# Seven groups per step, and narrow products of two units that alternate head by head

## The chip, the core and the metric

The kernel runs on one core of one Trainium2 chip. The metric is the device time of one execution in microseconds (us); less is better. Three runs of the kernel before gave a median of 929.04 us (928.44 to 930.88).

## What is computed

Inputs are q, k, v of shape (4, 8, 768, 48) (batch, heads, sequence, head dimension), beta of shape (4, 8, 768), and two weight matrices in double precision. The reference first runs the delta rule over the sequence, then a feed-forward over 3072 tokens of 384 features:

```python
k_n = k / (np.linalg.norm(k, axis=-1, keepdims=True) + 1e-06)
for t in range(S):
    y[:, :, t] = np.einsum('bhd,bhde->bhe', q[:, :, t], state)
    v_old = np.einsum('bhde,bhd->bhe', state, kt)
    state = state + bt[:, :, :, None] * np.einsum('bhd,bhe->bhde', kt, vt - v_old)
...
h = x @ w_in                              # 384 -> 2048
g = h * (1.0 / (1.0 + np.exp(-1.702 * h)))
out = (g @ w_out)                         # 2048 -> 384
```

## The kernel before

**Units and slots.** The sequence is cut into 6 chunks of 128 tokens. A *unit* is one chunk of one batch with all 8 heads; there are 24, in the order of chunks and, within a chunk, of the 4 batches. The main loop has 25 *slots*, and `slot(n, 20.8)` puts these works side by side: the second part of the step of unit n-1 (call it A) and the first part of the step of unit n (B), both from the generator `advance`; `prepare` for unit n+4; in pairs of slots one `invert` for two later units; in slots 0 to 3 the conversion of weights from double precision (`weights`); and some pieces of the feed-forward of finished units, 20.8 units of cost at 1.3 apiece, so 16 pieces. A pair of units makes 32 pieces, two slots' worth.

**A step.** A chunk is solved in 4 blocks of 32 rows. In `psR` stands what is to be taken from the values: for all rows the keys' products with the state `S_bd` (L421, four products of 128 x 96), and for block 1, 2 and 3 the products of the rows above, head by head (L430, 8 products of 32, 64 or 96 rows x 32 columns x 48). DVE subtracts the block of psR from the values `V` (L436). Then the 8 heads' block is multiplied with the inverse `XB` of the triangular system into `psU` (L438, 8 products of 32 x 32 x 48), and ACT copies it to `U` (L442). These L430 and L438 products are called narrow here, and eight of them in a row a burst. After block 3 come the new state's products (`psS`, L447), the queries' products with the old state and with U (`psY`, L456 and L462), ACT's copy to `x`, the state's update on DVE (L475), and the transposes of x into `psXT` (L481) and `xT` (L482).

**Around it.** `prepare` transposes k and q (`psT`, L285), forms the Gram matrices (`psG`, L299; rows 0 to 47 hold one head and 64 to 111 the next, and the two are multiplied in turn) and sends blocks of them through DRAM to `invert`, which inverts the triangular systems of two units on DVE (L339 to L397: a product, 15 rounds of a product and a sum, and 8 pairs of larger ones). `feed_forward` works pieces of three `ph` products (L495) for the first matrix and of two `po` products (L505) for the second. float32 products are two passes each on TensorE.

**What sets the order.** `merge` gives every work its number of items and a stretch of the slot, and takes the items in the order of their middles, one `yield` at a time. The framework then schedules each engine's instructions from that order and its own estimates; within one engine they run in the order that results. Buffers: `ps_seq` has four PSUM banks for psR, psU, psS, psY and psXT, so a fifth tile waits until one of the four has been read. While there is no feed-forward yet (slots 0 to 2), products on a constant keep TensorE busy (`warm`, L135; `warmth`: 8 times 4 per slot).

Of the kernel before, what the change touches and what calls it, by code (L numbers as in the profile page):

```python
# [8 lines left out]
F32 = mybir.dt.float32  # L9
# [3 lines left out]
ALU = mybir.AluOpType  # L13
ACT = mybir.ActivationFunctionType
# [4 lines left out]
def kernel(  # L19
# [31 lines left out]
    NB = C // BS  # L51
    HB = 2
# [76 lines left out]
    def warm(n, after=None):  # L129

        ps = ps_moe.tile([128, 256], F32, tag="moe", name="ps_warm")
        if after is not None:
            after(ps[:, 0:1], 0.0)
        for _ in range(n):
            nc.tensor.matmul(ps, lhsT=ones[:, 0:128], rhs=ones, start=True, stop=True)  # L135
# [272 lines left out]
        yield 0.0  # L408


    def advance(n, xT):
        c, b = units[n]
        kn, kqT, G = ready.pop(n)
        V = loaded.pop(n)
        XB = inverse.pop(n)
        psR = ps_seq.tile([128, H, D], F32, tag="seq", name="psR")
        psU = ps_seq.tile([128, H, D], F32, tag="seq", name="psU")
        U = wk.tile([128, H, D], F32, tag="U", name="U")
        if c > 0:
            for j in range(NP):  # L420
                nc.tensor.matmul(  # L421
                    psR[:, 2 * j : 2 * j + 2, :], lhsT=kqT[:, j, 0, :], rhs=S_bd[:, b, j],
                    start=(j == 0), stop=True, skip_group_check=True,
                )
            yield 1.0
        for blk in range(NB):
            r, above = slice(blk * BS, (blk + 1) * BS), slice(0, blk * BS)
            if blk > 0:
                for h in range(H):
                    nc.tensor.matmul(  # L430
                        psR[r, h, :], lhsT=G[above, h, 0, r], rhs=U[above, h, :],
                        start=(c == 0 and h == 0), stop=True, skip_group_check=True,
                    )
                yield 0.7
            if c > 0 or blk > 0:
                nc.vector.tensor_tensor(V[r], V[r], psR[r], op=ALU.subtract)  # L436
            for h in range(H):
                nc.tensor.matmul(  # L438
                    psU[r, h, :], lhsT=XB[r, h, :], rhs=V[r, h, :], start=True, stop=True
                )  # L440
            yield 0.7
            nc.scalar.copy(U[r], psU[r])  # L442

        if c < NC - 1:
            psS = ps_seq.tile([128, NP, 2, D], F32, tag="seq", name="psS")
            for j in range(NP):
                nc.tensor.matmul(  # L447
                    psS[:, j], lhsT=kn[:, 2 * j : 2 * j + 2, :].rearrange("p a d -> p (a d)"),
                    rhs=U[:, 2 * j : 2 * j + 2, :], start=True, stop=True,
                )  # L450

            yield 0.9
        psY = ps_seq.tile([128, H, D], F32, tag="seq", name="psY")
        if c > 0:
            for j in range(NP):
                nc.tensor.matmul(  # L456
                    psY[:, 2 * j : 2 * j + 2, :], lhsT=kqT[:, j, 1, :], rhs=S_bd[:, b, j],
                    start=(j == 0), stop=True, skip_group_check=True,
                )
            yield 0.9  # L460
        for h in range(H):
            nc.tensor.matmul(  # L462
                psY[:, h, :], lhsT=G[:, h, 1, :], rhs=U[:, h, :],
                start=(c == 0 and h == 0), stop=True, skip_group_check=True,
            )
            if h == 3:
                yield 0.9
        yield 0.9
        x = wk.tile([128, DM], F32, tag="o", name="x")
        nc.scalar.activation(x, psY.rearrange("p h d -> p (h d)"), ACT.Copy)  # L470

        if c < NC - 1:
            for hh in range(2):
                pr = slice(hh * 64, hh * 64 + 64)
                nc.vector.tensor_tensor(  # L475
                    S_bd[pr, b, :, hh, :], psS[pr, :, hh, :], S_bd[pr, b, :, hh, :], op=ALU.add
                )

        psX = ps_seq.tile([128, KC, 128], F32, tag="seq", name="psXT2")
        for j in range(KC):  # L480
            nc.tensor.transpose(psX[:, j, :], x[:, j * 128 : (j + 1) * 128], ident)  # L481
        nc.vector.tensor_copy(xT[:, :, b % HB * C : (b % HB + 1) * C], psX)  # L482
        yield 0.5


    def feed_forward(c, b0, xT):
# [47 lines left out]
    def warmth(n, k):  # L534
        for _ in range(n):
            warm(k)
            yield 0.0
# [11 lines left out]
    def merge(*works):  # L549

        order = sorted(
            (lo + (hi - lo) * (i + 0.5) / n, w)
            for w, (_, n, lo, hi) in enumerate(works) for i in range(n)
        )
        for _, w in order:
            next(works[w][0], None)
        for work, *_ in works:
            run(work)

    def run(work):  # L560
        for _ in work:
            pass

    def part(work, n):
        for _ in range(n):
            yield next(work, None)

    steps, xTs, inverting = {}, {}, {}

    def slot(n, share):  # L570

        c, b = units[n] if n < len(units) else (NC, 0)
        works = []
        if n > 0:
            works.append((steps.pop(n - 1), 8 if n > B else 7, 0.0, 1.0))
        if n < len(units):
            h = n // HB
            if b % HB == 0:
                xTs[h] = wk.tile([128, KC, NTH], F32, tag="xT", name="xT", bufs=3)
            steps[n] = advance(n, xTs[h])  # L580
            first = 5 if c > 0 else 3
            works.append((part(steps[n], first), first, 0.0, 1.0))
        if n + B < len(units):
            works.append((prepare(n + B), 4, 0.0, 1.0))
        m = n - HB
        if m >= 0 and m + B < len(units):
            if m % HB == 0:
                c1, b1 = units[m + B]
                inverting[0] = invert(c1, b1, HB)
                works.append((part(inverting[0], 13), 13, 0.3, 1.0))  # L590
            else:
                works.append((inverting[0], 13, 0.0, 0.65))
        if n < len(WB):
            works.append((weights(WB[n]), WB[n], 0.0, 1.0))
        if queue:
            works.append((take(share), max(1, round(share / 1.3)), 0.0, 1.0))
        elif n <= HB:
            works.append((warmth(8, NB0), 8, 0.0, 1.0))
        merge(*works)
        if n == len(WB) - 1:  # L600
            run(weights(n_parts))
        if n > 0:
            if n - 1 + B < len(units):
                load_values(n - 1 + B)
            m = n - 1 + len(KN)
            if m < len(units):
                load(m, ((KN, k), (QP, q)), sync if c == 0 else nc.sync.dma_start)
# [66 lines left out]
```

## Time and profile before

| | before |
|---|---|
| median of 3 runs | 929.04 us |
| the profiled execution | 928.69 us |
| its span on the core | 927.0 us |
| TensorE (PE): busy, passes | 877.7 us, 6356 |
| VectorE (DVE) busy | 495.4 us |
| ScalarE (ACT) busy | 195.4 us |
| GpSimd (POOL) busy | 100.8 us |
| mean granted TensorE clock | 0.965 |

The span is what the core's instructions cover; 1.7 us of the execution lie around it. PE counts passes of products, PEld the loads of their weights. A group's row names line, engine, operation, output and inputs, shape and count, then busy time and mean length of one in ns, then the idle time of the engine ahead of them and what ended it. Passes overlap, so the mean length of one is more than its distance from the next.

### The profile page before, as it was taken

To read this page: it belongs to the slowest core of one execution; us is meant where nothing else is said; L and a number is where in the kernel's file an instruction comes from. 1 tells how busy PE (TensorE), PEld (TensorE's weight loads), DVE (VectorE), ACT (ScalarE), POOL (GpSimd) and SP (SyncE) were. 2 spreads that over 40 slices of the span, in tenths; PEclk is the share of its full clock that TensorE was granted. 3 is DMA by queue.
4 is the path that set the end of the run, shared out by engine and by line. 5 is a ranking of instruction groups with operands and counts; after the bars stand their busy time and mean duration, and the time that the engine had idled before them with its cause. 6 is when DMAs were issued, how large, how long until landed. Compare 5 with 4: busy or idle time off the path is not lost.

```text
span 927.0 us, 14851 instructions
## 1 busy us (share of the span) xinstructions
PE 877.7 (95%) x6356; PEld 666.5 (72%) x6356; DVE 495.4 (53%) x1022; ACT 195.4 (21%) x354; POOL 100.8 (11%) x92
## 2 busy tenths in 40 slices
PE   8119999999999999999999999999999999999998
PEld 7107778678768778768768768768768768778684
DVE  7898787987591482482383383384293283110000
ACT  4103423222112212212212212212212102112020
POOL 2111030111011021011021011011000000000000
PEclk9657969999999999999999999999999999999999
DMA  9844562422212212213113113113112101000000
GB/s 232 221 53 113 151 164 51 111 64 50 58 43 50 49 48 54 46 44 60 41 46 64 37 49 63 32 37 74 29 39 48 29 23 27 5 13 1 10 9 18
DMA packets 159299, 54.55 MB, mean 59 GB/s; under 512 B 127232, under 2 KB 154880, under 8 KB 159232
## 3 DMA queue, kind: packets, MB, share of 16 engines
q1 hardware_dynamic: 153104, 52.38, 24.4%
q10 hardware_dynamic: 6128, 1.21, 0.9%
q8 instruction: 50, 0.82, 0.4%
q14 instruction: 17, 0.14, 0.1%
HBM read 33.13 MB, written 20.45 MB: 58 GB/s over the span
## 4 chain that ended last, share of the span: by engine, by line
PE 87%; DVE 10%; POOL 1%; issue 1%; ACT 0%; DVEq 0%; POOLq 0%
PE ph L495 29%; PE po L505 24%; PE psU L438 7%; PE psR L430 6%; PE psG L299 5%; PE psY L462 4%; PE ps_warm L135 3%; PE psT L285 3%; DVE P L346 2%; PE psS L447 2%; PE psY L456 2%; PE psR L421 2%; DVE A L347 1%; DVE P L101 1%; POOL rn L242 1%; DVE YB L101 1%
## 5 line engine op out<-in xcount | busy, mean ns | idle before, releaser
L495 PE MATMUL ph<-xT,w_in 128*128 128x256 f32 x1152 | 282.1, 389 | 1.6 <-DVE xT L482 1.6
L505 PE MATMUL po<-w_out,gT 128*128 128x384 f32 x768 | 279.4, 497 | 0.0
L495 PEld LDWEIGHTS ph<-xT,w_in 128*128 128x128 f32 x1152 | 210.0, 191 | 34.8 <-ACT gT L500 3.0
L505 PEld LDWEIGHTS po<-w_out,gT 128*128 128x128 f32 x768 | 135.5, 190 | 71.2 <-issue 2.3
L436 DVE TENSOR_TENSOR V<-V,psR 32x384 f32<-32x384 f32 x92 | 50.6, 550 | 182.2 <-PE psR L430 128.2
L500 ACT ACTIVATE gT<-ph 128x512 f32<-128x512 f32 x96 | 57.3, 597 | 221.4 <-PE ph L495 221.4
L442 ACT COPY U<-psU 32x384 f32<-32x384 f32 x96 | 45.1, 470 | 195.3 <-PE psU L438 194.6
L438 PEld LDWEIGHTS psU<-V,XB 32*32 32x32 f32 x1536 | 67.5, 106 | 24.7 <-issue 12.1
L438 PE MATMUL psU<-V,XB 32*32 32x48 f32 x1536 | 77.7, 205 | 0.0
L135 PE MATMUL ps_warm<-ident 128*128 128x256 bf16 x236 | 35.9, 310 | 42.3 <-DVE ps_warm L101 39.2
L430 PEld LDWEIGHTS psR<-U,G 64*32 64x32 f32 (+2 forms) x1152 | 53.5, 108 | 28.5 <-issue 19.4
L307 DVE COPY G<-psG 128x512 f32<-128x512 f32 x44 | 30.4, 690 | 70.0 <-PE psG L299 69.3
L430 PE MATMUL psR<-U,G 64*32 64x48 f32 (+2 forms) x1152 | 63.3, 206 | 0.6 <-ACT U L442 0.6
L323 POOL TENSOR_SCALAR_AFFINE_SELECT G<-G 128x1024 f32<-128x1024 f32 x24 | 33.8, 1410 | 251.5 <-DVE G L307 101.5
L135 PEld LDWEIGHTS <-ident 128*128 128x128 bf16 x236 | 25.1, 111 | 49.5 <-DVE ps_warm L101 40.2
L299 PE MATMUL psG<-kqT 48*128 48x256 f32 x384 | 59.4, 403 | 0.3
L462 PEld LDWEIGHTS psY<-U,G 128*128 128x128 f32 x384 | 51.2, 196 | 6.8
L363 DVE TENSOR_TENSOR P<-NT,YB 64x2 f32<-64x2 f32 (+4 forms) x150 | 51.0, 340 | 4.6
L299 PEld LDWEIGHTS psG<-kqT 48*128 48x128 f32 x384 | 36.6, 186 | 20.6 <-issue 15.7
L238 POOL TENSOR_TENSOR ksq<-KN 128x384 f32<-128x384 f32 x18 | 16.8, 932 | 312.3 <-DMA KN<-in_k_dram 312.3
L367 DVE TENSOR_REDUCE YB<-P 64x2 f32<-64x2 f32 (+4 forms) x150 | 48.0, 320 | 4.4
L462 PE MATMUL psY<-U,G 128*128 128x48 f32 x384 | 48.9, 272 | 0.0
(78 smaller groups left out, 687.6 us busy)
## 6 DMA issues: line engine op xcount, KB each, us to landing
Nd<-G SPq DMA_DIRECT2D x24, 512.0 KB, 3.2
w_out<-in_moe_w_in_dram SPq DMA_DIRECT2D x12, 512.0 KB, 5.1
w_out<-in_moe_w_out_dram SPq DMA_DIRECT2D x14, 384.0 KB, 3.6
KN<-in_k_dram SPq DMA_DIRECT2D x24, 192.0 KB, 2.8
V<-in_v_dram SPq DMA_DIRECT2D x24, 192.0 KB, 3.0
out_dram<-o SPq DMA_DIRECT2D x24, 192.0 KB, 1.9
QP<-in_q_dram SPq DMA_DIRECT2D x21, 192.0 KB, 3.0
NT<-Nd SPq DMA_DIRECT2D x24, 128.0 KB, 2.5
```

The costliest lines, as they stand in the source:

```text
L135: nc.tensor.matmul(ps, lhsT=ones[:, 0:128], rhs=ones, start=True, stop=True)
L299: nc.tensor.matmul(ps[hh][:, i], lhsT=kqT[pr, g + i, 0, :], rhs=kqT[pr, g + i, :, :], start=True, stop=True,)
L363: tt(P, diag(Nf, i * BS, [[0, i], [1, i]]), diag(Yf, 0, [[BS, i], [1, i]]), op=ALU.mult,)
L367: red(diag(Yf, i, [[BS, i]]), P, axis=AX.X, op=ALU.add, negate=True)
L430: nc.tensor.matmul(psR[r, h, :], lhsT=G[above, h, 0, r], rhs=U[above, h, :], start=(c == 0 and h == 0), stop=True, skip_group_check=True,)
L436: nc.vector.tensor_tensor(V[r], V[r], psR[r], op=ALU.subtract)
L438: nc.tensor.matmul(psU[r, h, :], lhsT=XB[r, h, :], rhs=V[r, h, :], start=True, stop=True)
L442: nc.scalar.copy(U[r], psU[r])
L462: nc.tensor.matmul(psY[:, h, :], lhsT=G[:, h, 1, :], rhs=U[:, h, :], start=(c == 0 and h == 0), stop=True, skip_group_check=True,)
L495: nc.tensor.matmul(ph[:, u], lhsT=w_in[:, j, f * 128 : (f + 1) * 128], rhs=xT[:, j, :], start=(j == 0), stop=(j == KC - 1),)
L500: nc.scalar.activation(gT[-1][:, f0 % FQ : f0 % FQ + 2], ph, ACT.Gelu_apprx_sigmoid)
L505: nc.tensor.matmul(po, lhsT=gT[f // FQ][:, f % FQ, i * C : (i + 1) * C], rhs=w_out[:, f, :], start=(f == 0), stop=(f == FC - 1),)
```

## The change

`advance` becomes a class `Step` with a method for each group of products, and `slot` writes out seven groups by hand, with the rest of the slot's work dealt out behind each: two items of the inversion, a seventh of what is left of the weights, and feed-forward pieces until a seventh of what is left of the 20.8 is used up (3, 3 and then 2 each) or, while there is none, 6 warm products (NB0; 4 before, and 8 times).

```diff
-    NW, NA0, NY, NB0 = 80, 3, 48, 4
+    NW, NA0, NY, NB0 = 80, 3, 48, 6
...
+        def solve(self, blk, h):
+            r = slice(blk * BS, (blk + 1) * BS)
+            nc.tensor.matmul(
+                self.psU[r, h, :], lhsT=self.XB[r, h, :], rhs=self.V[r, h, :],
+                start=True, stop=True,
+            )
...
-        works = []
-        if n > 0:
-            works.append((steps.pop(n - 1), 8 if n > B else 7, 0.0, 1.0))
...
-        merge(*works)
+        for group in range(7):
+            if group == 0:
+                if A:
+                    for h in range(H):
+                        A.above(2, h)
+                    A.rest(2)
+                if B_:
+                    B_.keys()
+                    B_.rest(0)
+                next(P, None)
+            elif group == 1:
+                for h in range(H):
+                    if A:
+                        A.solve(2, h)
+                    if B_:
+                        B_.solve(0, h)
+                if A:
+                    A.solved(2)
+                if B_:
+                    B_.solved(0)
+                next(P, None)
+            elif group == 2:
+                if A:
+                    for h in range(H):
+                        A.above(3, h)
+                    A.rest(3)
+                    A.queries()
+            elif group == 3:
+                for h in range(H):
+                    if A:
+                        A.solve(3, h)
+                    if B_:
+                        B_.above(1, h)
+                if A:
+                    A.solved(3)
+                if B_:
+                    B_.rest(1)
+                next(P, None)
+            elif group == 4:
+                if B_:
+                    for h in range(H):
+                        B_.solve(1, h)
+                    B_.solved(1)
+                if A:
+                    A.state()
+                next(P, None)
+                run(P)
+            elif group == 5:
+                if A:
+                    A.outputs()
+            elif A:
+                A.transposed()
+            ahead_of(inverting, 2)
...
+            if queue:
+                for cost in take(todo / (7 - group)):
+                    todo -= cost
+            elif n <= HB:
+                warm(NB0)
```

`above` is the product with the rows above (L430 before, L438 after), `rest` DVE's subtraction (L436, now L446), `solve` the product with the inverse (L438, now L450), `solved` ACT's copy, `keys` and `queries` the products with the state (both L427 now), `state` the new state with its update, now in one place, `outputs` psY's products with U, `transposed` the transposes. `queries` comes right behind `rest(3)`; before, it came behind the new state's products. Block 2's product with the rows above moves from unit n's first part, at a slot's end, to the next slot's first group.

PE's order in the middle of the program, before: part of a slot with psR and psU bursts, each with feed-forward products (ph) around it. A row's x is the number of equal products that follow each other, and the psU row of 16 is eight of one unit and then eight of the other.

```order
L430 MATMUL psR<-U,G 32x48 x8
L495 MATMUL ph<-xT,w_in 128x256 x6
L438 MATMUL psU<-V,XB 32x48 x16
L495 MATMUL ph<-xT,w_in 128x256 x3
L285 MATMUL psT<-ident,QP_83 128x128 x4
L495 MATMUL ph<-xT,w_in 128x256 x3
L447 MATMUL psS<-U,KN_75 128x96 x4
L495 MATMUL ph<-xT,w_in 128x256 x3
L430 MATMUL psR<-U,G 32x48 x8
L495 MATMUL ph<-xT,w_in 128x256 x3
L456 MATMUL psY<-S_bd,kqT 128x96 x4
```

Now, from the end of the second group into the fourth of a slot in the middle, with the numbers of the buffers (psU_3258 and psR_3257 are unit A's, psU_3513 and psR_3512 unit B's):

```order
L450 MATMUL psU_3258<-V_2763,XB_2993 32x48
L450 MATMUL psU_3513<-V_3017,XB_3470 32x48
L285 MATMUL psT_3566<-ident_106,QP1_83 128x128 x4
L515 MATMUL po_3541<-w_out_202,gT_3336 128x384 x2
L515 MATMUL po_3541<-w_out_202,gT_3406 128x384 x4
L438 MATMUL psR_3257<-U_3259,G_2428 32x48 x8
L515 MATMUL po_3541<-w_out_202,gT_3477 128x384 x2
L427 MATMUL psY_3593<-S_bd_117,kqT_2312 128x96 x4
L515 MATMUL po_3541<-w_out_202,gT_3477 128x384 x2
L450 MATMUL psU_3258<-V_2763,XB_2993 32x48
L438 MATMUL psR_3512<-U_3514,G_2667 32x48
```

The bursts' heads alternate between two units, the feed-forward stands in fewer and longer pieces, and psY with the state has moved ahead of psS, two po products behind the psR burst of block 3.

DVE's order around the subtractions of a slot with an inversion, before (the rounds of the inversion are L363 and L367, the larger products L346, `o` is the feed-forward's output):

```order
L363 TENSOR_TENSOR P<-NT,YB 64x338
L512 COPY o<-po 128x384
L436 TENSOR_TENSOR V<-V,psR 32x384
L367 TENSOR_REDUCE YB<-P 64x2x13
L363 TENSOR_TENSOR P<-NT,YB 64x392
L475 TENSOR_TENSOR S_bd<-psS,S_bd 64x4x48 x2
```

Now:

```order
L367 TENSOR_REDUCE YB<-P 64x2x14
L446 TENSOR_TENSOR V<-V,psR 32x384
L363 TENSOR_TENSOR P<-NT,YB 64x450
L367 TENSOR_REDUCE YB<-P 64x2x15
L346 TENSOR_TENSOR P<-NT,YB 64x1024
L346 TENSOR_TENSOR P<-NT,YB 64x768
L522 COPY o<-po 128x384
L446 TENSOR_TENSOR V<-V,psR 32x384
```

Block 3's subtraction stands behind 14 rounds of the inversion, all of them since block 0's, and block 1's behind the last round, two larger products and the copy of `o`.

More of the change, by code (lines that the diff above doesn't have):

```diff
@@ L420, in advance @@
             for j in range(NP):
                 nc.tensor.matmul(
-                    psR[:, 2 * j : 2 * j + 2, :], lhsT=kqT[:, j, 0, :], rhs=S_bd[:, b, j],
-                    start=(j == 0), stop=True, skip_group_check=True,
-                )
[L425 to L436, printed above, removed]
+                    ps[:, 2 * j : 2 * j + 2, :], lhsT=self.kqT[:, j, i, :],
@@ new lines, in queries, with state @@
+        def queries(self):
+            self.psY = self.bank("psY")
+            if self.c > 0:
+                self.with_state(self.psY, 1)
+        def state(self):
+            if self.c == NC - 1:
+                return
+            psS = self.bank("psS", (128, NP, 2, D))
+            for j in range(NP):
+                nc.tensor.matmul(
+                    psS[:, j],
+                    lhsT=self.kn[:, 2 * j : 2 * j + 2, :].rearrange("p a d -> p (a d)"),
+                    rhs=self.U[:, 2 * j : 2 * j + 2, :], start=True, stop=True,
+                )
+            for hh in range(2):
+                pr = slice(hh * 64, hh * 64 + 64)
+                St = S_bd[pr, self.b, :, hh, :]
+                nc.vector.tensor_tensor(St, psS[pr, :, hh, :], St, op=ALU.add)
@@ L437, in advance, with outputs @@
+        def outputs(self):
             for h in range(H):
                 nc.tensor.matmul(
-                    psU[r, h, :], lhsT=XB[r, h, :], rhs=V[r, h, :], start=True, stop=True
-                )
[L441 to L481, printed above, removed]
@@ L576, in slot @@
         if n < len(units):
             h = n // HB
-            if b % HB == 0:
+            if n % HB == 0:
                 xTs[h] = wk.tile([128, KC, NTH], F32, tag="xT", name="xT", bufs=3)
[L580 to L584, printed above, removed]
-        m = n - HB
[L586 to L598, printed above, removed]
-        merge(*works)
+            B_ = steps[n] = Step(n, xTs[h])
+        P = prepare(n + B) if n + B < len(units) else iter(())
+        m = n - HB
+        if m >= 0 and m % HB == 0 and m + B < len(units):
+            inverting = invert(*units[m + B], HB)
@@ new lines, in slot @@
+        left = WB[n] if n < len(WB) else 0
+        todo = share
+        for group in range(7):
[51 more added lines that the diff above has]
+            ahead_of(inverting, 2)
+            more = left // (7 - group)
+            run(weights(more))
+            left -= more
+            if queue:
[3 more added lines that the diff above has]
+                warm(NB0)
```

76 lines of the change are left out of this document (47 added, 29 removed).

## The prediction, made before the changed kernel ran

> **What bounds the kernel now.** I read the page first: busy time, then the slices.
>
> ```profile
> PE 877.7 (95%) x6356; PEld 666.5 (72%) x6356; DVE 495.4 (53%) x1022; ACT 195.4 (21%) x354; POOL 100.8 (11%) x92
> PE   8119999999999999999999999999999999999998
> DVE  7898787987591482482383383384293283110000
> PEclk9657969999999999999999999999999999999999
> ```
>
> PE is full from the fourth slice on, at the full clock from the seventh; DVE is half free behind it. The busy times by window, for one stretch of the start and one two-slot stretch of the middle (length, then busy time and count per engine, then clock, DMA share, GB/s):
>
> ```profile
> core 0: us, PE busy (x) PEld busy (x) DVE busy (x) ACT busy (x) POOL busy (x), PEclk, DMA share, GB/s
> 106.00:132.00 26.00, 24.16 (x229) 19.26 (x226) 21.64 (x55) 9.51 (x18) 5.31 (x5) 0.77 0.60 144
> 415.00:485.00 70.00, 70.00 (x518) 53.04 (x517) 36.69 (x74) 14.61 (x27) 9.34 (x8) 1.00 0.21 46
> ```
>
> In the middle PE has work in all 70.00 us. What is gained there must come out of PE's own instructions. A busy PE can still be draining or waiting for weights, so I next looked at PE's timeline around some short products ("busy" runs from the first start to the last end; the next row starts before that end):
>
> ```profile
> 494.06 1.40 PE L438 MATMUL psU<-V,XB 32*32 32x48 f32 x32
> ...
> 496.79 0.60 PE L285 MATMUL psT<-ident,QP 128*128 128x128 f32 x4
> 497.23 1.46 PE L495 MATMUL ph<-xT,w_in 128*128 128x256 f32 x6
> ...
> 499.39 1.49 PE L495 MATMUL ph<-xT,w_in 128*128 128x256 f32 x6
> 500.80 0.86 PE L430 MATMUL psR<-U,G 32*32 32x48 f32 x16
> 501.60 1.56 PE L495 MATMUL ph<-xT,w_in 128*128 128x256 f32 x6
> 503.00 1.03 PE L456 MATMUL psY<-S_bd,kqT 128*128 128x96 f32 x8
> 503.86 1.27 PE L495 MATMUL ph<-xT,w_in 128*128 128x256 f32 x5
> ```
>
> Every float32 product is two passes (x16 is 8 heads); a transpose is one. The pace of a feed-forward pass, and of two slots, comes from the chain of waits (start, length, work):
>
> ```profile
> 170.62 4.52 PE po L505 x14
> ...
> 205.14 6.48 PE ph L495 x30
> 211.62 1.33 PE psU L438 x32
> ...
> 282.37 1.33 PE psU L438 x32
> ```
>
> A ph pass takes 6.48 / 30 = 0.216 us, a po pass 4.52 / 14 = 0.323; the same burst comes back after two slots, 70.8 us. From 499.39 to 503.00 there are 3.61 us, of which twelve such passes are 2.59; so **a burst of 8 narrow products costs 1.02 us** with its way in and out. Its own passes: (0.86 - 0.20) / 15 = 0.044 us apart, taking 0.20 us for the last pass from the groups below, so some 0.70 us is passing and 0.32 us is the way in and out. A burst of 16 products, A's eight and then B's eight, is busy 1.40 instead of 0.86: 0.54 us more, hence **1.56 us**. That is less than sixteen more passes at 0.044 (0.70): where the second unit's products, in other rows and columns of the array, follow the first's, some passes ran beside each other.
>
> ```profile
> L438 PE MATMUL psU<-V,XB 32*32 32x48 f32 x1536 | 77.7, 205 | 0.0
> L430 PE MATMUL psR<-U,G 64*32 64x48 f32 (+2 forms) x1152 | 63.3, 206 | 0.6 <-ACT U L442 0.6
> ```
>
> The narrow products hold PE for 141 us of 927, and more with the switching.
>
> **Does taking turns work?** The change has the heads of two units alternate over the whole burst. The nearest thing in the trace is psG, whose heads alternate between rows 0 to 47 and 64 to 111 of the array already:
>
> ```profile
> 505.28 1.13 PE L299 MATMUL psG<-kqT 48*128 48x256 f32 x8
> L299 PE MATMUL psG<-kqT 48*128 48x256 f32 x384 | 59.4, 403 | 0.3
> ```
>
> Eight passes of 256 columns, the size of a ph pass, start within 1.13 - 0.40 = 0.73 us, 0.10 apart on average, where ph's are 0.216 apart. Two groups of rows each run at the full pace when their products alternate in fours of load and pass. I carry that over to the narrow bursts: 16 alternating products last as long as 8, plus one small offset: **1.03 us**, an estimate from the 1.02 row. Its passes are five times shorter than psG's, and that is what the first rival is about.
>
> **The burst term.** Counted over PE's whole order, before: 122 bursts of 8, 23 of 16. After: 90 of 8 and 39 alternating ones (21 of two units' block solves, 18 of a solve with the other unit's block product; in the first slots the scheduler has pulled some pairs apart). Before 122 x 1.02 + 23 x 1.56 = 160.3; after 90 x 1.02 + 39 x 1.03 = 132.0. **-28.3 us**, nearly all of it on the path, since PE sets the end.
>
> **Small wide groups** (psR, psY and psS of four products, the transposes). They lie less often behind feed-forward passes, and more often behind a burst or each other. A burst's way out is already in the 1.02. What is left is that their first weights aren't loaded under a long pass. The psY group above, behind a ph pass, takes 0.86 us (503.00 to 503.86), 0.108 a pass. I put a quarter of a pass, 0.03 us, on two groups in each of 20 slots: **+1.2**, an estimate, bounds 0 and 3.
>
> **Warm-up products.** Slots 0 to 2 get 7 x 6 instead of 8 x 4, 30 more.
>
> ```profile
> L135 PE MATMUL ps_warm<-ident 128*128 128x256 bf16 x236 | 35.9, 310 | 42.3 <-DVE ps_warm L101 39.2
> ```
>
> 35.9 / 236 = 0.152 each, 4.6 us if all stand on the path, 0 if all fall into waits of the first steps; I take **+2.3**.
>
> **The wait for xT.**
>
> ```profile
> L495 PEld LDWEIGHTS ph<-xT,w_in 128*128 128x128 f32 x1152 | 210.0, 191 | 34.8 <-ACT gT L500 3.0 <-DVE xT L482 2.6 <-DVE P L363 0.7
> ```
>
> Where a new pair of units enters the feed-forward, ph waits 2.6 us in all for the copy of xT. After, the transposes are the seventh group, and behind them come four po products, block 2's burst, the state product and the transposes of the next step (8 x 0.323 + 1.02 + 0.86 + 0.44 = 4.9 us) before the first ph. **-2.6**, bounds -2.6 and 0.
>
> **The wait that is added.** psY's products with the state now stand two ph (or po) products behind block 3's burst, and take a fifth bank of a pool of four, the one that psR has until DVE's subtraction has read it. All of PE queues behind that psY. The pace without DVE being late, from the timeline of DVE behind the 500.80 burst:
>
> ```profile
> 501.70 0.55 DVE L436 TENSOR_TENSOR V<-V,psR 32x384 f32<-32x384 f32 x1 [9.77 <-PE psR L430]
> ```
>
> It ended at 502.25, 0.65 after the next ph's start at 501.60. Two ph products are four passes, 0.86 us; two po products 1.29. So 0 us, with 0.2 us to spare behind ph and 0.6 behind po. If DVE comes late that cover is gone; the case is below. The other hand-overs to DVE and ACT have two or three pieces behind them, 2.6 us and more. That XB is ready: as before, DVE's order has a pair's whole inversion done a slot ahead of its use; the loads moved past on SP stay as many as they were and cost nothing.
>
> **The start.** Slots 0 to 3 hang on the steps' own hand-overs, on weight conversion in DVE (21.64 of 26.00 us above) and on a clock of 0.77. Seven strict groups may go better or worse there: 26 x 0.23 = 6 us is what a full clock would give; I take 0, bounds -6 and +6.
>
> **Sum.** -28.3 + 1.2 + 2.3 - 2.6 = -27.4. The profiled execution took 928.7 (span 927.0 and 1.7 around it): 901.3. The median of the runs is 0.35 above it: **901.6 us**. With all bounds at their good ends -36.9, 892; at their bad ends -14.7, 914.
>
> **Rivals.** *Passes come too slowly to fill two row groups.* The fastest sequence of narrow passes that the trace holds is the second half of the x32 burst, 0.54 / 16 = 0.034 us on average. If that were the least spacing, an alternating burst would be busy 0.20 + 31 x 0.034 = 1.25 us instead of 0.87: 39 x 0.38 = 14.8 more, 916. For it: nothing here shows 32 narrow passes at 0.022. Against it: psG's heads come in the same turns, loads and passes of one before those of the other, and still run level. 0.14.
> The Trainium skill has a rule of this kind (TensorE: Matmul & The Clock Gate, "Wait — 56ns, not 53.3ns?"): starts never come closer than some 25 ns however short the product; an estimate by it is 39 x 32 x 3 ns = 4 us more, 905. The x32 row neither bears it out nor excludes it.
>
> *Alternating gains no more than standing side by side.* Then the 39 cost 1.56: 39 x 0.53 = 20.7 more, 922. Against it psG. 0.06.
>
> *DVE becomes the bound in every second slot, and the time is longer.* One pair's inversion is worked in one slot:
>
> ```profile
> L363 DVE TENSOR_TENSOR P<-NT,YB 64x2 f32<-64x2 f32 (+4 forms) x150 | 51.0, 340 | 4.6
> L367 DVE TENSOR_REDUCE YB<-P 64x2 f32<-64x2 f32 (+4 forms) x150 | 48.0, 320 | 4.4
> L346 DVE TENSOR_TENSOR P<-A,NT 64x256 f32<-64x256 f32 (+3 forms) x40 | 33.6, 861 | 1.2
> L346 DVE TENSOR_TENSOR P<-NT,YB 64x1024 f32<-64x1024 f32 (+3 forms) x40 | 33.4, 858 | 0.3
> L347 DVE TENSOR_REDUCE YB<-P 64x64 f32<-64x256 f32 (+3 forms) x40 | 31.6, 810 | 0.4
> L347 DVE TENSOR_REDUCE A<-P 64x64 f32<-64x1024 f32 (+3 forms) x40 | 31.5, 810 | 0.4
> L397 DVE TENSOR_TENSOR YS<-YB,bI 64x1024 f32<-64x1024 f32 (+1 forms) x11 | 13.4, 1216 | 0.2
> L339 DVE TENSOR_TENSOR NT<-NT,bI 64x1024 f32<-64x1024 f32 x10 | 12.2, 1219 | 0.3
> ```
>
> 229.1 / 10 + 1.2 + 1.2 = 25.3 us of the 36.7 in two slots; with half of the rest, 31.0 us in a slot that shall shrink from 35.4 to about 33.9. There are ten such slots, all with po pieces. The decisive place is block 3's subtraction, ahead of psY. From block 0's subtraction on DVE has 14 rounds, at most 14 x 0.66 = 9.2 us; PE has 24 po passes (7.8), two groups of transposes (0.9) and two bursts (2.05), 10.7, less some 0.8 until block 0's subtraction is done: 9.9. Only 0.7 to spare, and the 0.6 behind po. If DVE came 2.7 us later than that cover allows in each of the ten slots, the 27.4 would be gone; from there on it is slower than before, 932 with 3 us. For it: the small margins and an in-order queue. Against it: 31.0 is under 33.9, and before, with as much to do in 35.4, V mostly found DVE waiting:
>
> ```profile
> L436 DVE TENSOR_TENSOR V<-V,psR 32x384 f32<-32x384 f32 x92 | 50.6, 550 | 182.2 <-PE psR L430 128.2
> ```
>
> 0.07.
>
> *The time does not move, or the groups don't come as written* (the scheduler undoes them, or the start loses what the middle gains): the order shows the turns in 39 bursts, so 0.03.
>
> **Numbers.** The forecast as worked out has 0.70. The range goes from 890, a little below the good ends, to 917, which takes in the 914 and the slow feed's 916; outside lie the side-by-side case, the two last and a remnant, some 0.17. A measurement of this kernel tells about 0.3% (2.8 us) from no change. Faster by more: 0.70 + 0.14 + 0.06, less a little for a start gone badly, 0.88; within it 0.03; slower 0.09.
>
> **What would show it.** Right: in the timeline after, psU bursts of x32 busy about 0.9 us instead of 1.40; two slots in about 67.7 us where they took 70.8; the narrow groups' busy time near 112 us (90 x 0.86 + 39 x 0.87) where it was 141; no waits of psY on V. Slow feed: x32 bursts of 1.0 to 1.25. DVE bound: idle time of PE's psY or psU put down to V in every second slot, and DVE without idle time ahead of V there. Wrong altogether: two slots of 70 us or more with x32 bursts at 1.4.

## The result, and the profile after

| | before | after |
|---|---|---|
| median | 928.74 us (4 runs, 925.15 to 930.88) | 891.23 us (4 runs, 887.91 to 894.75) |
| profiled execution, its span | 928.69, 927.0 us | 889.75, 888.0 us |
| mean granted clock | 0.965 | 0.974 |

The ratio is 0.960 (95% interval 0.955 to 0.965): 37.5 us less by the medians, 39.0 by the two spans. The forecast was 901.6, range 890 to 917.

From the page of the changed kernel, busy times and then the slices of DVE and of the clock:

```profile
PE 841.3 (95%) x6386; PEld 638.2 (72%) x6386; DVE 491.2 (55%) x1022; ACT 194.8 (22%) x354; POOL 99.8 (11%) x92
DVE  7889689978781771671681681681681570110000
PEclk9659999999999999999999999999999999999999
```

PE still sets the end. Two things differ: its clock is at 90% or more (a 9) in every slice from the fourth on, where before it was so from the seventh, and DVE's full and empty slots alternate more sharply in the middle (6 to 8 and 1, before 8 and 2 to 4).

The stretches of the start and of the middle that were shown of before, and then two stretches of a slot's length, the first with most of an inversion:

```profile
core 0: us, PE busy (x) PEld busy (x) DVE busy (x) ACT busy (x) POOL busy (x), PEclk, DMA share, GB/s
106.00:132.00 26.00, 26.00 (x280) 21.58 (x280) 21.14 (x61) 12.23 (x21) 7.23 (x6) 1.00 0.69 182
415.00:485.00 70.00, 70.00 (x552) 53.29 (x550) 38.02 (x76) 15.79 (x29) 9.39 (x8) 1.00 0.22 50
424.00:458.00 34.00, 34.00 (x252) 23.81 (x251) 26.32 (x57) 6.49 (x12) 4.89 (x4) 1.00 0.17 41
458.00:491.60 33.60, 33.60 (x271) 27.54 (x270) 10.99 (x18) 8.23 (x15) 5.00 (x5) 1.00 0.30 63
```

In the same 70 us PE starts 552 passes where it started 518, and DVE has 26.32 us of work in the stretch with most of the inversion, 10.99 in the other. The chain of waits gives the period of two slots:

```profile
363.45 3.87 PE po L515 x12
...
430.54 3.87 PE po L515 x12
```

The same po pieces come back after 67.09 us (70.8 before). Why is seen in PE's timeline, through the second, third and the beginning of the fourth group of one slot:

```profile
501.44 0.87 PE L450 MATMUL psU<-V,XB 32*32 32x48 f32 x32
...
506.69 0.87 PE L438 MATMUL psR<-U,G 96*32 96x48 f32 x16
507.49 1.56 PE L515 MATMUL po<-w_out,gT 128*128 128x384 f32 x4
508.89 1.03 PE L427 MATMUL psY<-S_bd,kqT 128*128 128x96 f32 x8
...
511.61 0.20 PE L450 MATMUL psU<-V,XB 32*32 32x48 f32 x1
511.62 0.20 PE L438 MATMUL psR<-U,G 32*32 32x48 f32 x1
511.65 0.20 PE L450 MATMUL psU<-V,XB 32*32 32x48 f32 x1
511.66 0.20 PE L438 MATMUL psR<-U,G 32*32 32x48 f32 x1
```

The psU burst of 32 passes at 501.44 is busy 0.87 us where it was 1.40; sixteen passes of one unit alone (506.69) take the same 0.87. The last four rows are the inside of an alternating burst: a pass of unit A and a pass of unit B start 0.01 us apart, and the next two 0.04 later, so each unit goes at its own 0.04 and they go side by side.

Where the 39 us went is read from the first and last start of the feed-forward passes. The rows of ph and po seen by tile (count, least, median and longest ns, first and last start in us), first of before:

```profile
L495 PE MATMUL ph<-xT,w_in x1152: 379/379/793, 132.1 to 902.7; 128*128 128x256 f32 x192
L505 PE MATMUL po<-w_out,gT x768: 486/486/590, 166.4 to 923.2; 128*128 128x384 f32 x192
```

and of after:

```profile
L505 PE MATMUL ph<-xT,w_in x1152: 378/379/484, 123.1 to 863.7; 128*128 128x256 f32 x192
L515 PE MATMUL po<-w_out,gT x768: 485/486/591, 156.6 to 884.2; 128*128 128x384 f32 x192
```

From the first ph to the last po it is 791.1 us before and 761.1 after: **-30.0**. The first ph comes 9.0 us earlier: **-9.0**. From the last po to the span's end it is 3.8 in both.

### The profile page after: what moved, and what is told of

Read it like the earlier page. It is cut to its first block, busy times and chain, and to the rows that moved or that the text cites. A ratio compares the mean times of both kernels' runs of the same rounds, so it can differ in the third digit from the quotient of the medians.

```text
span 888.0 us, 14915 instructions
## 1 busy us (share of the span) xinstructions
PE 841.3 (95%) x6386; PEld 638.2 (72%) x6386; DVE 491.2 (55%) x1022; ACT 194.8 (22%) x354; POOL 99.8 (11%) x92
## 4 chain that ended last, share of the span: by engine, by line
PE 93%; DVE 5%; DMA 1%; issue 0%; POOL 0%; ACT 0%; SPq 0%; DVEq 0%
PE ph L505 29%; PE po L515 29%; PE psU L450 7%; PE psG L299 6%; PE psR L438 5%; PE psY L481 5%; PE ps_warm L135 3%; PE psT L285 3%; PE psS L469 2%; PE psR L427 2%; PE psY L427 2%; DVE P L101 1%; PE psXT L491 1%; DVE YB L101 1%; DVE z L101 1%; DVE tmp L101 1%
## 5 line engine op out<-in xcount | busy, mean ns | idle before, releaser
L505 PE MATMUL ph<-xT,w_in 128*128 128x256 f32 x1152 | 268.2, 383 | 0.0
L515 PE MATMUL po<-w_out,gT 128*128 128x384 f32 x768 | 268.0, 493 | 0.0
L446 DVE TENSOR_TENSOR V<-V,psR 32x384 f32<-32x384 f32 x92 | 50.7, 551 | 167.3 <-PE psR L438 160.1
L450 PEld LDWEIGHTS psU<-V,XB 32*32 32x32 f32 x1536 | 54.7, 105 | 30.6 <-issue 19.0
L438 PEld LDWEIGHTS psR<-U,G 64*32 64x32 f32 (+2 forms) x1152 | 52.6, 107 | 21.3 <-issue 20.0
L323 POOL TENSOR_SCALAR_AFFINE_SELECT G<-G 128x1024 f32<-128x1024 f32 x24 | 29.0, 1210 | 338.5 <-DVE G L307 180.0
L450 PE MATMUL psU<-V,XB 32*32 32x48 f32 x1536 | 64.9, 203 | 0.0
L438 PE MATMUL psR<-U,G 64*32 64x48 f32 (+2 forms) x1152 | 62.3, 205 | 0.0
L363 DVE TENSOR_TENSOR P<-NT,YB 64x2 f32<-64x2 f32 (+4 forms) x150 | 48.7, 325 | 4.8 <-DVE YB L367 0.3
L367 DVE TENSOR_REDUCE YB<-P 64x2 f32<-64x2 f32 (+4 forms) x150 | 48.0, 320 | 4.7
L481 PEld LDWEIGHTS psY<-U,G 128*128 128x128 f32 x384 | 46.9, 193 | 3.6
L493 DVE COPY xT<-psXT 128x384 f32<-128x384 f32 x24 | 13.2, 552 | 64.1 <-PE psXT L491 64.0
L286 ACT ACTIVATE kqT<-psT 128x512 f32<-128x512 f32 x48 | 27.9, 593 | 85.5 <-PE psT L285 85.4
L481 PE MATMUL psY<-U,G 128*128 128x48 f32 x384 | 45.5, 272 | 0.0
L522 DVE COPY o<-po 128x384 f32<-128x384 f32 x24 | 13.3, 555 | 53.8 <-PE po L515 53.4
```

The costliest lines, as they stand in the source:

```text
L363: tt(P, diag(Nf, i * BS, [[0, i], [1, i]]), diag(Yf, 0, [[BS, i], [1, i]]), op=ALU.mult,)
L367: red(diag(Yf, i, [[BS, i]]), P, axis=AX.X, op=ALU.add, negate=True)
L438: nc.tensor.matmul(self.psR[r, h, :], lhsT=self.G[a, h, 0, r], rhs=self.U[a, h, :], start=(self.c == 0 and h == 0), stop=True, skip_group_ ...
L446: nc.vector.tensor_tensor(self.V[r], self.V[r], self.psR[r], op=ALU.subtract)
L450: nc.tensor.matmul(self.psU[r, h, :], lhsT=self.XB[r, h, :], rhs=self.V[r, h, :], start=True, stop=True,)
L481: nc.tensor.matmul(self.psY[:, h, :], lhsT=self.G[:, h, 1, :], rhs=self.U[:, h, :], start=(self.c == 0 and h == 0), stop=True, skip_group_ ...
```

## The experiments

All kernels do the whole computation. Except for e4 and e9, which change the kernel before, each changes the changed kernel. "First to last" is from the first ph to the last po of the profiled execution. The half clock is worked out from the windows, twice (1 - PEclk) times 20 us, over 75 to 135 us.

| | median us (runs) | first ph | last po | first to last | half clock |
|---|---|---|---|---|---|
| before | 928.74 (4) | 132.1 | 923.2 | 791.1 | 22.0 |
| after | 891.23 (4) | 123.1 | 884.2 | 761.1 | 3.6 |
| e1_side | 913.41 (4) | 126.4 | 907.7 | 781.3 | 10.4 |
| e2_cool | 905.27 (4) | 139.2 | 899.9 | 760.7 | 38.8 |
| e3_side_cool | see there | 139.0 | 926.4 | 787.4 | |
| e4_warm_before | 928.34 (10) | 130.5 | 923.0 | 792.5 | 10.4 |
| e5_by2 | 894.69 (2) | 123.1 | 885.0 | 761.9 | 3.6 |
| e6_by4 | 899.40 (2) | 123.1 | 893.8 | 770.7 | 3.6 |
| e7_split | 898.67 (2) | 121.4 | 890.9 | 769.6 | 0 |
| e8_swap | 887.32 (6) | 122.8 | 882.1 | 759.3 | 3.6 |
| e9_before40 | 932.02 (10) | 133.2 | 925.9 | 792.7 | 16.4 |
| e10_swap_warm8 | 891.10 (4) | 126.8 | 884.9 | 758.1 | 0 |

The first theory: the 30 us of the middle are the forecast's terms, the turns above all. Its rival: the turns are worth little, and the regrouping or something else gives the gain. For the 9 us of the start the question was whether the clock gives them, and what gives the clock.

**e1: the seven groups stay, the turns go.** In the second and fourth group, A's eight products and then B's eight:

```diff
-                for h in range(H):
+                for h0 in range(0, H, 8):
                     if A:
-                        A.solve(2, h)
+                        for h in range(h0, h0 + 8):
+                            A.solve(2, h)
                     if B_:
-                        B_.solve(0, h)
+                        for h in range(h0, h0 + 8):
+                            B_.solve(0, h)
...
```

> The changed kernel with the turns undone: in the second and fourth group unit A's eight products come first and then unit B's eight; all else as changed. Theory 1 (the turns bring the gain): each of the 39 bursts costs 1.56 us again instead of about 1.03, so 20.7 us more than 891.2, about 912. Rival (the seven groups with longer feed-forward stretches bring it, the turns little): not over 896.

Measured 913.41 us (910.20 to 915.82), 0.982 of before (0.978 to 0.986). The rows of ph and po by tile:

```profile
L505 PE MATMUL ph<-xT,w_in x1152: 378/379/484, 126.4 to 887.2; 128*128 128x256 f32 x192
L515 PE MATMUL po<-w_out,gT x768: 485/486/591, 160.4 to 907.7; 128*128 128x384 f32 x192
```

Its timeline in the middle:

```profile
514.28 1.40 PE L450 MATMUL psU<-V,XB 32*32 32x48 f32 x32
```

The burst is back at 1.40, and first to last is 781.3, **20.2 us** more than after (the forecast: 20.7; by the medians it is 22.2, since the first ph comes 3.3 us later too, with 10.4 us of half clock in place of 3.6). So the turns are worth 20.2 of the 30.0 us in the middle, and the rest of the change, with 16 bursts fewer (145 to 129) and no wait for xT, 791.1 - 781.3 = **9.8** (the forecast: 28.3 - 20.7 - 1.2 + 2.6 = 9.0). The first theory holds.

**e2: fewer warm products, about as many as before.**

```diff
-                warm(NB0)
+                warm(4 + group % 2)
```

> The changed kernel with 4 or 5 warm products behind a group, 31 in a slot as against 42 (32 before the change). Theory 2 (more warm products keep the TensorE clock up in the first slots, and that gave what the forecast had at 0): the trace shows half clock for 10 to 20 us again between 85 and 137 us, and the time rises by 5 to 10 us, to 896 to 901. Rival (the seven groups hand over faster whatever the clock): within 3 us of 891.

Measured 905.27 (904.62 to 909.23), ratio 0.974 (0.971 to 0.978): 14.0 over after, more than was expected. First to last is after's, 760.7; all of it lies in the start, whose windows show the granted clock in the third column behind the length:

```profile
core 0: us, PE busy (x), PEclk, DMA share, GB/s
95.00:115.00 20.00, 20.00 (x141) 0.53 0.43 114
115.00:135.00 20.00, 20.00 (x127) 0.50 0.26 58
```

PE is as busy as ever, at half the clock. The seven groups with 31 warm products per slot do worse in the start than the order of before with 32; with 42 they do far better. The extra warm products, forecast as a cost of 2.3, are a gain of 14 in this order, by the medians.

**e3: e1 and e2 together,** to see whether the two gains add up.

```diff
-                for h in range(H):
+                for h0 in range(0, H, 8):
...
-                warm(NB0)
+                warm(4 + group % 2)
```

> Both undone: no turns, and 31 warm products in a slot. If the two parts add, 20.7 + 5 to 10 above 891.2: 917 to 922, and what is left to the 928.7 of before is the regrouping alone, 7 to 12 us. Rival (they don't add, since without turns PE is busier and stays warm): about 912, as with the turns alone undone.

The four runs, 910.4, 925.7, 931.5 and 932.0 us, had mean clocks of 0.973, 0.956, 0.949 and 0.949, so that their median (928.59) isn't used. The one at 0.973 took about as long as e1 (913.41, its four at 0.970 to 0.976): in that run, which has no trace, 31 warm products did not cost e2's 14 us. So their number doesn't settle by itself whether the clock drops. In the profiled run, the one of 932.0 us, a second stretch at half clock, about 208 to 222 us, lengthens first to last to 787.4. Counting feed-forward passes in the trace, from the 271st to the last one it is 667.9 us, as in e1 (before 678.8, after 649.2). So behind the start the two changes don't touch each other; for the whole time e3 is inconclusive.

**e4 and e9: the kernel before, with more warm products.** If their number alone sets the clock, the order of before should win those 9 us too.

```diff
-    NW, NA0, NY, NB0 = 80, 3, 48, 4
+    NW, NA0, NY, NB0 = 80, 3, 48, 6
```

> The kernel before with 6 instead of 4 products at each of the 8 warm places, 48 in a slot. Theory 2 (the clock): full clock from about 100 us on, and 5 to 10 us less than 928.7: 919 to 924. Rival (the groups, not the clock, made the start shorter): the same time or up to 4 us more for 48 more products.

e9 has 5 in place of 6, so 40 per slot, near after's 42.

```diff
-    NW, NA0, NY, NB0 = 80, 3, 48, 4
+    NW, NA0, NY, NB0 = 80, 3, 48, 5
```

> The kernel before with 5 instead of 4 products at each of its 8 warm places, 40 in a slot against 42 in the changed kernel. Theory (the number of warm products alone sets the clock and with it the first feed-forward pass): half clock under 10 us in all between 75 and 140 us, the first feed-forward pass at 123 to 126 us, 6 to 9 us less than 928.7. Rival (it takes the seven groups as well, since with 48 the order of before still came to its first pass only at 130.5): first pass at 129 to 132, the time within 3 us of before.

e4 measured 928.34 (ratio 0.998, 0.996 to 1.001), e9 932.02 (1.004, 1.001 to 1.006). No gain in either. The window from 115 to 135 us, of before:

```profile
115.00:135.00 20.00, 18.16 (x118) 0.62 0.58 135
```

of e4:

```profile
115.00:135.00 20.00, 19.37 (x140) 0.74 0.47 107
```

of e9:

```profile
115.00:135.00 20.00, 19.01 (x132) 0.59 0.39 94
```

and of after:

```profile
115.00:135.00 20.00, 20.00 (x182) 1.00 0.71 188
```

The number alone falls as a theory. In the timeline the last warm products and the first ph stand like this in e9:

```profile
115.17 0.72 PE L135 MATMUL ps_warm<-ident 128*128 128x256 bf16 x5
...
133.17 1.22 PE L495 MATMUL ph<-xT,w_in 128*128 128x256 f32 x2
```

and in after:

```profile
121.11 0.82 PE L135 MATMUL ps_warm<-ident 128*128 128x256 bf16 x6
...
123.14 4.05 PE L505 MATMUL ph<-xT,w_in 128*128 128x256 f32 x18
```

In e9 (and before) 17 us of short products and small waits follow the last warm product, and the clock is down in them; the new code deals six out behind every group, to 1.2 us before the first ph. Some of e4's come as late as 125.8, and it still has 0.74, so "late enough" isn't the whole condition either.

**e5 and e6: turns of two and of four heads.** If PE only has to see both units' products somewhere ahead, all are equal; if only a few passes can wait while the other unit's go on, by fours loses most.

```diff
-                for h in range(H):
+                for h0 in range(0, H, 2):
                     if A:
-                        A.solve(2, h)
+                        for h in range(h0, h0 + 2):
+                            A.solve(2, h)
...
```

This is e5, in both groups as in e1; e6 has 4 in place of 2.

> The changed kernel with turns of two heads instead of one (A's two, B's two, and so on), all else the same. Theory (PE lets some passes of the one unit wait in their rows while it passes on those of the other; before, B's first pass ran beside the last three of A): four passes in a turn fit nearly, so the alternating psU burst takes 0.80 to 0.87 us to the next group, and from the first feed-forward pass to the end at most 2 us more than after. Rival (products run side by side however far apart they stand): exactly as after. Rival (only strict turns of one head work): 8 us and more.

> Turns of four heads. Theory of few waiting passes: eight passes in a turn no longer fit, so a part of each turn runs alone; the alternating psU burst takes 1.0 to 1.1 us, and from the first feed-forward pass to the end it is 8 to 11 us more than after. Rival (any distance): as after. Rival (only one head): as with A's eight and B's eight, 20 us more.

e5 measured 890.52 and 898.85, e6 899.32 and 899.47 (ratios 0.962, 0.955 to 0.969, and 0.967, 0.961 to 0.973). Two runs each decide little; the traces do. One burst in the timeline of e5:

```profile
501.77 0.89 PE L450 MATMUL psU<-V,XB 32*32 32x48 f32 x32
```

and one in that of e6:

```profile
505.98 1.12 PE L450 MATMUL psU<-V,XB 32*32 32x48 f32 x32
```

All 39 alternating bursts of a trace last the same, in both 0.02 us over the upper end of what was expected. First to last grows by 0.8 us for twos and 9.6 for fours, where 39 bursts of 0.25 us more make 9.8. With all 32 passes one behind the other a burst would take 0.87 + 16 x 0.042 = 1.54 us, an estimate from the row of 16 passes (506.69, after) and from what its second eight add to e7's row of eight below, (0.87 - 0.53) / 8. With one change of unit it is 1.40, with three 1.12: each change lets 0.14 us pass side by side, some three passes. The fourth group of a slot of e6 shows them, A's psU and B's psR; the program has eight passes of A first, then eight of B:

```profile
515.96 0.40 PE L450 MATMUL psU<-V,XB 32*32 32x48 f32 x5
516.15 0.23 PE L438 MATMUL psR<-U,G 32*32 32x48 f32 x1
516.19 0.20 PE L450 MATMUL psU<-V,XB 32*32 32x48 f32 x1
...
516.28 0.20 PE L450 MATMUL psU<-V,XB 32*32 32x48 f32 x1
```

B's first pass starts behind five of A's, and A's last three (516.19, 516.24, 516.28) start after it. The theory of few waiting passes holds. By it the estimate is 0.56 for seven changes, below the 0.87 that one unit needs by itself, which is why twos (0.89) are nearly as good as ones (0.87).

**e7: one burst cut in two,** block 3's product with the rows above, with a feed-forward piece between the halves. It measures what a way into and out of a burst costs.

```diff
                     for h in range(H):
+                        if h == H // 2 and queue:
+                            todo -= next(queue[0], 0) or 0
                         A.above(3, h)
```

> The changed kernel with block 3's burst cut in two halves of four heads with one feed-forward piece between them. Theory of the forecast's sum (a burst's way in and out costs 0.32 us): in about 20 slots one more way in and out, so 6 to 8 us more from the first feed-forward pass to the end. Rival (the way in and out is hidden, only passes count): 0.

Measured 896.44 and 900.90. In the timeline the cut burst stands as

```profile
509.30 0.53 PE L438 MATMUL psR<-U,G 96*32 96x48 f32 x8
509.76 1.56 PE L515 MATMUL po<-w_out,gT 128*128 128x384 f32 x4
511.25 0.53 PE L438 MATMUL psR<-U,G 96*32 96x48 f32 x8
```

First to last is 8.5 us more for 21 cut bursts. The list of waits of PE has 1.5 us of this, which after doesn't have (0.8 for xT, 0.7 for V). The other 7.0 are 0.33 us for each cut; the forecast had 0.32. The term holds.

**e8: one change of kind less.** In the fifth group the psG product is placed ahead of the state's products, beside the burst, since both use parts of the array.

```diff
                 if B_:
                     for h in range(H):
                         B_.solve(1, h)
                     B_.solved(1)
+                next(P, None)
                 if A:
                     A.state()
-                next(P, None)
                 run(P)
```

> The changed kernel with the second psG group moved between block 1's burst and psS, so that PE changes the shape of its tiles three times there instead of four. Theory (each change of shape costs 0.1 to 0.2 us): 20 slots times 0.1 to 0.2, so 2 to 4 us less, 887 to 889. Rival (psG's banks or its copies make PE wait there, or DVE gets the state later): no gain, or a loss of 2 to 5 us.

The median is 887.32 (6 runs, 886.89 to 892.76), ratio 0.955 (0.951 to 0.959), the best of all kernels; its interval overlaps that of after, so the medians alone don't settle it. Runs at the same mean clock do better: at 0.977 it is 886.89 to 887.07 us against 887.91, at 0.971 890.62 against 892.71, at 0.969 892.76 against 894.75. First to last is 1.8 us less. One place in the timeline, from that burst to the next feed-forward product, with the state's products and psG between them; of after:

```profile
515.80 0.86 PE L450 MATMUL psU<-V,XB 32*32 32x48 f32 x16
...
518.72 0.59 PE L515 MATMUL po<-w_out,gT 128*128 128x384 f32 x1
```

and of e8:

```profile
514.66 0.86 PE L450 MATMUL psU<-V,XB 32*32 32x48 f32 x16
...
517.49 1.80 PE L515 MATMUL po<-w_out,gT 128*128 128x384 f32 x5
```

From the burst to the next po it is 2.92 us and 2.83: 0.09 for a change less. (Both views end at 519, so the counts of their last rows are not whole.) In some 20 slots that is the 1.8.

**e10: e8 with eight warm products per group,** for the last stretch of half clock.

```diff
-    NW, NA0, NY, NB0 = 80, 3, 48, 6
+    NW, NA0, NY, NB0 = 80, 3, 48, 8
```

> The changed kernel with the second psG group behind block 1's burst, and 8 instead of 6 warm products behind each group. Theory (the clock sets the start, and what is left of half clock is 0 to 3.4 us): full clock throughout, worth at most 1.5 us, against 14 more products in each of three slots, 0 to 4 us: the first pass at 121 to 126 us and the time 886 to 891. Rival (the warm products stand on the path one by one): 4 us more than with 6.

Measured 891.10 (890.41 to 892.76), ratio 0.960 (0.955 to 0.965). The clock is full in all three windows, and still the last po comes 2.8 us later than in e8. In the timeline behind the last warm products:

```profile
120.94 1.04 PE L135 MATMUL ps_warm<-ident 128*128 128x256 bf16 x8
...
125.42 0.70 PE L299 MATMUL psG<-kqT 48*128 48x256 f32 x4 [0.69 <-ACT kqT L286]
126.76 1.56 PE L505 MATMUL ph<-xT,w_in 128*128 128x256 f32 x6 [0.63 <-DVE xT L493]
```

In size this is the rival's 4 us (3.8 by the medians), but not as it was put. The warm products end at 121.98, 0.40 behind e8's 121.58; the other 3.6 of the 4.0 us by which the first ph is later come behind them. There the schedule comes out otherwise: a burst, transposes and psG stand ahead of the first ph, with waits of 0.69 and 0.63 us. Eight are worse than six here.

## Why the prediction was right, and where it was off

**What bounds the kernel** was right. After 130 us PE has no wait of any kind in the list of waits (before it had 1.6 us, all for xT); the rest of what was gained in the middle came out of its own instructions.

**The burst term** (-28.3, of it 20.7 by the turns) was right in mechanism and size: 20.2 by e1, and together with the small groups (+1.2) and xT (-2.6) it was to be -29.7, and is -30.0. It isn't spread evenly, though: from the first ph to the 271st feed-forward pass both kernels take 112 us (132.1 to 244.4 and 123.1 to 235.0), and all the gain lies behind that, where two slots gain 3.7 us (70.8 to 67.09) and not the 3.1 of the forecast. That psG, with passes of 256 columns, could stand in for passes of 48 was the bold step, and it held.

**The sign for the narrow groups' busy time** was stated badly. It was to be near 112 us; the rows of the groups give more:

```profile
L450 PE MATMUL psU<-V,XB 32*32 32x48 f32 x1536 | 64.9, 203 | 0.0
L438 PE MATMUL psR<-U,G 64*32 64x48 f32 (+2 forms) x1152 | 62.3, 205 | 0.0
```

The sum is 127.2. In the 18 bursts where psU of one unit alternates with psR of the other, the same 0.86 us counts in both groups; without 18 x 0.86 = 15.5 it is 111.7.

**Small wide groups** (+1.2, bounds 0 and 3) weren't isolated. **The wait for xT** is gone, as forecast, but it was smaller than the -2.6: that number stood in the row of the weight loads, and PE itself waited 1.6 us, by its own row of before:

```profile
L495 PE MATMUL ph<-xT,w_in 128*128 128x256 f32 x1152 | 282.1, 389 | 1.6 <-DVE xT L482 1.6
```

**The added wait of psY on V** was to cost nothing, with 0.6 us to spare behind po. In DVE's timeline the subtraction of block 3 in the slot shown above is

```profile
507.60 0.56 DVE L446 TENSOR_TENSOR V<-V,psR 32x384 f32<-32x384 f32 x1 [0.60 <-PE psR L438]
```

It ends at 508.16, and psY starts at 508.89: 0.73 to spare. DVE had itself been idle for 0.60 us ahead of it, so the rival in which DVE is late did not come about. Its 31.0 us of DVE work per inversion was right: from the first instruction of the one at 426.28 (L339) to the end of its last at 463.34 (L397) DVE is busy for 31.0 us. What was wrong is that this stays within one slot of about 33.9: it takes 37.1 us, and some 4.5 us of the inversion lie in the second of the two stretches shown above. DVE had 6.1 us free meanwhile, and nothing on PE waited for it.

**The rivals of the feed.** The forecast's least spacing of 0.034 us doesn't exist: (0.87 - 0.20) / 31 = 0.0216 us between passes. The Trainium skill (TensorE: Matmul & The Clock Gate, "Wait — 56ns, not 53.3ns?") has starts never closer than about 25 ns; here they are 21.6 ns apart on average, and some only 10 by the rows above. That sentence and the measurement differ, and the measurement decides: the floor doesn't hold between products in different rows and columns of the array.

**The start** is the step that failed: 0 with bounds of -6 and +6, and 2.3 on top for the warm products; measured -9.0 for both. The bound of -6 came from the window of 106 to 132 us alone; the 6.8 us of half clock between 75 and 95 us, where the clock was 0.83 (the row below), were not in it. The forecast took the clock as something that the change leaves alone on average, and the warm products as a cost. They were neither. The windows before the first ph, of before

```profile
75.00:95.00 20.00, 19.86 (x188) 0.83 0.37 89
95.00:115.00 20.00, 20.00 (x239) 1.00 0.57 164
```

and of after

```profile
75.00:95.00 20.00, 19.73 (x229) 1.00 0.45 116
95.00:115.00 20.00, 20.00 (x230) 0.91 0.51 135
```

give, with the two from 115 us shown above, 22.0 us of half clock before and 3.6 after. Among the kernels with the seven groups the first ph comes at 121.4, 123.1, 126.4 and 139.2 us for 0, 3.6, 10.4 and 38.8 us of it, some 0.46 us per us (e10, with its other order, isn't among them). By that the clock is worth 18.4 x 0.46 = 8.5 of the 9.0. That is an estimate, and in e2 the number of warm products differs too.

The runs without a trace bear it out, since one kernel's mean clock differs from run to run. The kernel before took 924.94 to 925.09 us in four runs at 0.969, and 937.30 and 937.40 in two at 0.954: 12.3 us for 28.8 us more of half clock (twice (1 - clock) times the span), 0.43 us per us in one and the same order. The changed kernel took 887.91 at 0.977 and 894.75 at 0.969, 6.8 us for 14.6, so 0.47. At the same clock of 0.969 the change is worth 925.0 - 894.75 = 30.3 us, about the 30.0 of the middle, and what is left of the 39.0 goes with the clock. At 0.969 there is a single run of the changed kernel, and where the half clock lay is not seen in runs without a trace.

Why more warm products in the old order bought some clock and gained no time shows in part in e9: at 0.969 six runs of e9 took 931.35 to 932.73, over 6 us more than the kernel before at that clock. Its 24 extra passes, at the forecast's 0.152 us, are 3.6 us; what the rest is isn't shown. Nor is why the clock drops where it does. Shown is that all four runs of the new order without its extra warm products lose 13 us or more (e2), and that about as many or more in the old order gain nothing.

**The range.** 891.23 lies inside it by 1.2 us, and two of the four runs lie below 890. With all bounds at their good ends the forecast came to 892. That the measurement is still inside owes to an end set 2 us lower, and with the start as it came out this was luck.

## What to carry to other kernels

Where TensorE is full of small products in different rows and columns of the array, let them alternate, one or two products at a time: here turns of one head gained 20.2 us, turns of four only half of it. Gather short products into fewer bursts, since each way into and out of one costs about 0.33 us here. And when the order of the work ahead of the steady state changes, look at the granted clock there window by window, and read products that only keep the engine busy as a price and a gain at once, tried both up and down.

## What the runs showed of the hardware that was not expected

- Passes of two units' products start about 0.01 us apart, 0.0216 on average over 32 of them, in float32 and with a load of weights for each.
- Only some three passes of one unit run beside the other's at each change of unit (1.40 us with one change, 1.12 with three, 0.89 with seven, 0.87 with fifteen), and there the trace shows passes that start ahead of earlier ones of the program (e6).
- PE can be busy in 20.00 of 20.00 us and have a granted clock of 0.50 (e2, from 115 to 135 us): being busy with short products did not keep the clock up. With 42 warm products per slot in place of 31 it was 1.00 in the same window; in one run of e3 the mean clock was 0.973 with 31 too.
- Runs of one kernel differ in their mean clock, and each us more at half clock cost some 0.43 (before) to 0.47 us (after), an estimate from their times.
